# Six of the first layer's weight pieces staged in the tail of the second layer's weights, with a new order for the begin

## The chip, the cores and the metric

The kernel runs on one core of a Trainium2 chip. The metric is the device time of one execution in microseconds (us); three runs of the kernel before gave 632.26, 632.70 and 633.21, median 632.7. The profile is one further execution, of 632.08 us.

## The reference, cut to what matters

A delta-rule attention over 4 batches and 8 heads (768 steps, 48 wide) feeds a two-layer network over its 3072 tokens.

```python
for t in range(S):                                    # 768 steps
    y[:, :, t] = einsum('bhd,bhde->bhe', q[:, :, t], state)
    v_old = einsum('bhde,bhd->bhe', state, k_n[:, :, t])
    state = state + beta_t * einsum('bhd,bhe->bhde', k_n[:, :, t], v[:, :, t] - v_old)
x = y.transpose(0, 2, 1, 3).reshape(3072, 384)
h = x @ w_in                                          # 384 -> 2048
out = (h * cos(h)) @ w_out                            # 2048 -> 384
```

The two weights come as float64.

## The kernel before

**Attention.** The 768 steps are 24 *units* of 32 steps, each for all 32 pairs of batch and head. A unit n is a chain of *tasks*, and the state links unit n to n + 1. Its loads are `k n`, `q n` and `v n` (four DMAs of 48 KB each to unit 7; from unit 8 on `k n` has eight of half the size, and the q and k blocks for the turn come separately). Then: norms of k (`square` on ScalarE (ACT), `sum` on VectorE (DVE), `norms`, a power, on GpSimd (POOL), `scale` on DVE), `turn` (transposes on TensorE (PE), L561; copied out by `turn_out` on ACT), `gram` (PE, L598), read by `gram_keys`, `fold` and `gram_queries` on DVE; the inverse of a unit triangular matrix, for two units at once, in pieces `inv(m, i)` on POOL (L734, L735), for the first two units on DVE, between `cross` and `back` on DVE; `state` (PE, L764); `old` (ACT, L776); `right` (DVE, L787 and L791); for units 0 to 3 `solve_half` (PE, L801), `half_out` (ACT), `between` (PE, L801), `between_out` (DVE, L819), `solve` (PE, L835), for later units only `solve` (L841); `solve_out` (DVE, L849); `update` of the state (PE, L862) and `update_out` (DVE, L870 or L872); `within` (PE, L879), copied out by `within_out` (ACT, L897) and, for units 0 to 3, `within_rest` (DVE, L895); `features`, a transpose (PE, L905), and `features_out` (ACT, L912). From unit 4 on `within_turn` (DVE), `within_put` and `features_out` (both DMAs) take the place of the last two. `busy` tasks are 26 small multiplications (L954) that only keep PE at work in the begin.

**The network.** Two units make a block p of 256 tokens; there are twelve. Blocks 0 and 1 form h by `hidden(p, f)` in eight steps of two halves each (PE, L963, 12 instructions a half); `hidden(0, 0)` needs the first three pieces of w_in, `hidden(0, 6)` all twelve. Each step is gated by `turns` (ACT, L1001), `rest` (DVE, L1008), `cos` (ACT, L1017) and `gate` (DVE, L1026). Block 0 is multiplied by w_out in `out(0, i, k)` (PE, L1169), which need four more pieces of w_out for each k. From block 2 on the first layer goes through sums of x and of weight blocks (`x_sum`, `in_sums` on DVE; `layer`, PE, L1149), and from block 1 on the second through seven products (L1226) with sums of weights (`right(x, e)`, DVE, L1255; not to be taken for the `right` of a unit) and of gates (`left`). `store` is the DMA of a result.

**The weights.** They come in 28 *pieces*: 0 to 11 are w_in (128 x 512 words of 8 bytes, 512 KB each), 12 to 27 w_out (128 x 384, 384 KB, one tile f each). Piece t passes through `weights t` (the load, on SyncE's queue (SP), L454), `split t` (two operations on ACT, L462 and L464), `shift t` (two on DVE, L468 and L473) and `add t` (one on POOL, L477), which makes float32 of it in w_in or w_out. The raw words lie in one of four places, w0 to w3, until their add is done; a load takes the place that came free first.

**What sets the order.** `Order.LINE` lists all 2253 tasks by number. `run` calls them in that order, so each engine and SP's queue get their instructions in the order of the list, and an instruction at the head waits for what it needs while all behind it on its engine wait too. Every DMA on SP also waits until the eighth DMA before it has landed. PSUM banks go in the same way: three for hidden (`h`), one shared (`two`) by turn, gram, the solves, update and features, one (`kq`) for state and within, and for turn and gram of units 1 and 3.

Of the kernel before, what the change touches and what calls it, by code (L numbers as in the profile page):

```python
# [12 lines left out]
U32 = mybir.dt.uint32  # L13
# [187 lines left out]
def kernel(  # L201
# [36 lines left out]
    DM = H * D  # L238
# [1571 lines left out]
```

## Time and profile before

| | us |
|---|---|
| median of three runs | 632.7 |
| the profiled execution | 632.08 |
| its span, first to last instruction | 630.3 |
| PE busy | 601.7 (95%) |
| DVE busy | 546.2 (87%) |
| ACT busy | 352.3 |
| POOL busy | 348.3 |
| mean granted PE clock | 0.985 |

The profile cuts the span into 40 slices of 15.76 us; a digit is an engine's busy share of a slice in tenths. A line of PE, DVE or ACT in order of time has its start, its duration, the source line, what is written and read, and in brackets how long the engine sat idle before it and what ended that wait; "issue" means that the profile shows nothing the engine waited for. SPq is SP's queue; its waits are listed with their total, number and longest.

### The profile page before, as it was taken

The page shows a single profiled execution, that of the slowest core. Times are in us where ns is not written, and L with a number is a line of the kernel's source. Part 1 is how long each engine was busy: PE and PEld are TensorE (multiplying, and loading weights), DVE is VectorE, ACT ScalarE, POOL GpSimd, SP SyncE. Part 2 cuts the span into 40 slices and gives each one's busy share as a digit, 9 for nine tenths or more (in the row PEclk, how much of TensorE's full clock was granted, in tenths as well). Part 3 has the DMA queues.
Part 4 walks back from the last instruction along what each step waited for, and adds up shares of the span by engine and source line. Part 5 has one row for each costly group of instructions (what it writes and reads, how often), then busy time and mean ns, then how long its engine had stood idle before and what let it go on. Part 6 is the DMA issues. An engine that isn't in the chain of part 4 may idle for free.

```text
span 630.3 us, 24280 instructions
## 1 busy us (share of the span) xinstructions
PE 601.7 (95%) x10096; PEld 558.2 (89%) x10096; DVE 546.2 (87%) x1131; ACT 352.3 (56%) x643; POOL 348.3 (55%) x703
## 2 busy tenths in 40 slices
PE   7678899999999999999999999999999999999997
PEld 5557778876999999999999999999999999999996
DVE  7998878999999999998898989989989787878872
ACT  3647566653455755656556656645646645746340
POOL 4467687868758588384286882782683860000000
PEclk9879799999999999999999999999999999999999
DMA  9887474764455645555446335644323203110000
GB/s 184 186 221 175 134 167 111 133 97 88 80 99 96 111 76 103 103 91 103 83 77 132 66 56 110 102 85 86 78 64 81 45 14 65 35 43 21 1 27 25
DMA packets 223986, 57.62 MB, mean 91 GB/s; under 512 B 215684, under 2 KB 218900, under 8 KB 223876
## 3 DMA queue, kind: packets, MB, share of 16 engines
q1 hardware_dynamic: 221444, 55.22, 43.1%
q8 instruction: 80, 1.31, 0.9%
q10 hardware_dynamic: 2176, 0.39, 0.4%
q0 software_dynamic: 256, 0.45, 0.3%
q14 instruction: 30, 0.25, 0.1%
HBM read 42.13 MB, written 13.89 MB: 89 GB/s over the span
## 4 chain that ended last, share of the span: by engine, by line
PE 80%; DVE 8%; DMA 4%; ACT 2%; issue 2%; SPq 2%; POOL 1%; DVEq 0%; ACTq 0%; POOLq 0%
PE p_out L1226 29%; PE p_h L1149 28%; PE p_kq L764 4%; PE p_h L963 3%; PE p_out L1169 3%; PE p_s L862 3%; PE p_kq L879 3%; PE p_g L598 3%; PE p_u L841 2%; DMA pairs<-in_moe_w_in_dram 2%; PE p_o L1226 2%; DMA qp<-in_q_dram 1%; SPq L339 1%; DVE p_h L1047 1%; DVE pairs L468 1%
## 5 line engine op out<-in xcount | busy, mean ns | idle before, releaser
L734 POOL TENSOR_TENSOR part<-z,gb 128x56 f32<-128x56 f32 (+25 forms) x325 | 134.7, 414 | 107.0 <-DMA gb<-g_dr 67.0
L735 POOL TENSOR_TENSOR z<-z,part 128x56 f32<-128x56 f32 (+25 forms) x325 | 140.3, 432 | 25.5
L1165 ACT COPY g_ffn<-p_h 128x512 f32<-128x512 f32 x140 | 80.2, 587 | 91.8 <-DVE p_h L1047 47.4
L1226 PE MATMUL p_out<-w_out,g_ffn 128*128 128x192 f32 x672 | 121.2, 329 | 0.0
L1047 DVE TENSOR_TENSOR p_h<-p_h,g_ffn 128x512 f32<-128x512 f32 x140 | 97.0, 695 | 21.3 <-PE p_h L1149 13.3
L1226 PEld LDWEIGHTS p_out<-w_out,g_ffn 128*128 128x128 f32 x672 | 107.8, 190 | 1.2 <-issue 0.2
L1001 ACT ACTIVATE turns<-p_h,quarter_turn 128x512 int32<-128x512 f32 x96 | 65.8, 688 | 65.5 <-DVE p_h L1047 54.8
L1226 PE MATMUL p_out<-w_sum,g_ffn 128*128 128x192 f32 x496 | 90.8, 331 | 0.0
L1017 ACT ACTIVATE turns<-turns,halfpi 128x512 f32<-128x512 f32 x96 | 69.1, 722 | 38.6 <-DVE turns L1008 37.0
L1149 PE MATMUL p_h<-x_sum,w_in 128*128 128x128 f32 x640 | 83.4, 277 | 0.3 <-ACT g_ffn L1165 0.2
L1226 PEld LDWEIGHTS p_out<-w_sum,g_ffn 128*128 128x128 f32 x496 | 79.5, 190 | 1.6 <-DVE o L1276 0.4
L1149 PEld LDWEIGHTS p_h<-x_sum,w_in 128*128 128x128 f32 x640 | 78.1, 192 | 1.6 <-ACT g_ffn L1165 0.9
L1008 DVE SCALAR_TENSOR_TENSOR turns<-p_h,turns 128x512 f32<-128x512 f32 x96 | 65.1, 682 | 7.2 <-ACT turns L1001 6.6
L1026 DVE TENSOR_TENSOR g_ffn<-turns,p_h 128x512 f32<-128x512 f32 x86 | 58.3, 679 | 8.1 <-ACT turns L1017 8.0
L1242 DVE TENSOR_TENSOR g_ffn<-g_ffn 128x512 f32<-128x512 f32 x88 | 62.2, 716 | 3.7 <-PE p_out L1226 3.5
L1149 PE MATMUL p_h<-x_sum,in_sum 128*128 128x128 f32 x400 | 53.6, 277 | 0.3 <-DVE g_ffn L1026 0.3
L897 ACT COPY y<-p_kq 32x384 f32<-32x384 f32 x88 | 41.4, 470 | 22.1 <-PE p_kq L879 16.6
L1149 PEld LDWEIGHTS p_h<-x_sum,in_sum 128*128 128x128 f32 x400 | 49.5, 192 | 1.2 <-DVE g_ffn L1026 0.6
L963 PE MATMUL p_h<-x_ffn,w_in 128*128 128x128 f32 x384 | 48.1, 280 | 1.1 <-ACT x_ffn L912 0.7
L963 PEld LDWEIGHTS p_h<-x_ffn,w_in 128*128 128x128 f32 x384 | 44.9, 193 | 2.7 <-POOL w_in L477 0.9
L776 ACT COPY rhs<-p_kq 32x384 f32<-32x384 f32 x86 | 40.2, 468 | 5.3 <-PE p_kq L764 2.8
L1149 PE MATMUL p_h<-x_ffn,w_in 128*128 128x128 f32 x320 | 42.8, 278 | 0.1
(133 smaller groups left out, 893.6 us busy)
## 6 DMA issues: line engine op xcount, KB each, us to landing
pairs<-in_moe_w_in_dram SPq DMA_DIRECT2D x12, 512.0 KB
pairs<-in_moe_w_out_dram SPq DMA_DIRECT2D x16, 384.0 KB
gb<-g_dr SPq DMA_DIRECT2D x20, 256.0 KB
vp<-in_v_dram SPq DMA_DIRECT2D x96, 48.0 KB
out_dram<-o SPq DMA_DIRECT2D x23, 192.0 KB
y_dr<-y_t SPq DMA_DIRECT2D x20, 192.0 KB
x_ffn<-y_dr SPq DMA_DIRECT2D x40, 96.0 KB
kp<-in_k_dram SPq DMA_DIRECT2D x128, 24.0 KB
```

Of the source, the lines that this page charges most:

```text
L734: eng.tensor_tensor(out=part, in0=row, in1=times, op=ALU.mult)
L735: eng.tensor_tensor(out=behind, in0=behind, in1=part, op=ALU.subtract)
L963: nc.tensor.matmul(p_h[:, i], w_in[:, t, (4 * k + i) * 128 : (4 * k + i + 1) * 128], moved(p, t, unit), start=(t == 0), stop=(t == KT - 1),)
L1001: nc.scalar.activation(turns[p, f], hidden_of(p, f), AF.Identity, bias=quarter_turn, scale=TURN)
L1008: nc.vector.scalar_tensor_tensor(out=r, in0=hidden_of(p, f), scalar=TURN, in1=t, op0=ALU.mult, op1=ALU.subtract,)
L1017: nc.scalar.activation(r, r, AF.Sin, bias=halfpi, scale=2.0 * math.pi)
L1026: nc.vector.tensor_tensor(out=place(p, f), in0=step_of(rests.pop((p, f)), f), in1=step_of(hidden_of(p, f), f), op=ALU.mult,)
L1047: nc.vector.tensor_tensor(out=out, in0=one, in1=two, op=ALU.add if op == "add" else ALU.subtract)
L1149: nc.tensor.matmul(p_h[:, e], in_block(w)[:, e], form(p, x), start=first and e == 0, stop=True, skip_group_check=True,)
L1165: nc.scalar.copy(block(p, *CHAIN[i][3]), p_hs[p, BANK[i]])
L1226: nc.tensor.matmul(p_o, left(p, part, a)[:, e % 4], right(e, b), start=(e == 0), stop=(e == FT // 2 - 1), skip_group_check=True,)
L1242: nc.vector.tensor_tensor(out=left(p, s, to), in0=left(p, s, one), in1=left(p, s, two), op=op)
```

## The change

**Staging.** Odd pieces of w_in (1, 3, 5, 7, 9, 11) no longer take one of w0 to w3. They are loaded into four places e0 to e3 of 1024 words per partition each, which are the last 4096 of the 6144 words of the w_out tile. These hold tiles f = 5 to 15 of w_out, written by pieces 17 to 27; `split` of these pieces now also waits for the adds of the six odd pieces.

**Order.** The tasks at places 17 to 1080 of the list stand in another order; ahead of them and behind them the list is the same. The last of them run at about 295 us in the profile of before. Each engine has the same tasks as before. In the begin the lists differ as follows (x:y for task x of unit, block or piece y):

| | before | after |
|---|---|---|
| SP | w0 k2 w1 q2 w2 k3 w3 q3 w4 k4 v0 w5 k5 w6 q4 w7 v1 w8 q5 w9 k6 w10 v2 w11 w12 v3 k7 q6 gram_put4 w13 w14 k8 w15 w16 w17 w18 | w0 k2 w1 k3 w2 q2 w3 q3 w4 k4 v0 w5 k5 w6 q4 w7 w8 v1 w9 k6 w10 k7 w11 q5 w12 k8 v2 w13 w14 q6 gram_put4 w15 v3 w16 w17 w18 |
| POOL | norms 0, add 0, 1, norms(1,0), add 3, norms(1,1), add 2, 4, 5, norms 2, add 7, 6, 8, inv(1,0-1), add 10, 12, inv(1,2), add 11, 9, inv(1,3), add 14, 13, norms 3, add 16, 15 | norms 0, norms(1,0), add 0, 3, 1, 2, norms(1,1), norms 2, add 4, 6, 5, 7, 8, 9, inv(1,0-1), add 10, inv(1,2), add 11, 12, inv(1,3), add 13, 14, norms 3, add 15, 17, 16 |
| DVE, from cross 0 | cross0 fold0 inv(0,0) gram_queries1 shift1 inv(0,1) sum(1,0) inv(0,2) fold1 shift3 shift2 inv(0,3) sum(1,1) scale(1,0) back0 gram_keys2 weigh(0,0) fold2 right0 gram_queries2 shift4 shift5 sum(2,0) between_out0 scale(1,1) solve_out0 shift6 shift7 weigh(0,1) update_out0 within_rest0 | cross0 sum(1,0) inv(0,0) fold0 inv(0,1) gram_queries1 inv(0,2) scale(1,0) shift3 shift1 fold1 inv(0,3) sum(1,1) shift2 back0 gram_keys2 weigh(0,0) fold2 right0 gram_queries2 sum(2,0) shift4 between_out0 shift5 solve_out0 shift6 shift7 update_out0 shift8 within_rest0 |
| DVE, on to update_out 1 | shift8 gram_keys3 cross1 scale(2,0) fold3 gram_queries3 shift9 gram_keys4 shift10 gram_queries4 shift12 right1 shift11 rest(0,0) rest(0,2) between_out1 gate(0,0) solve_out1 sum(3,0) weigh(1,0) shift14 update_out1 | scale(1,1) gram_keys3 shift9 gram_queries3 fold3 cross1 shift10 scale(2,0) sum(3,0) gram_keys4 gram_queries4 weigh(0,1) rest(0,0) right1 shift11 gate(0,0) shift12 between_out1 solve_out1 rest(0,2) shift14 shift13 update_out1 |
| ACT, around old 1 | features_out0 split10 split9 old1 split12 turns(0,2) turns(0,0) split11 square3 half_out1 cos(0,0) | split9 features_out0 eye2 split10 square3 old1 split12 turns(0,0) split11 cos(0,0) half_out1 |
| PE | turn2, six busy, turn3, five busy, gram2 ... within0 busy turn4 gram3 busy features0 hidden(0,0) state1 gram4 hidden(0,2) hidden(0,4) solve_half1 | turn2, six busy, gram2, turn3 ... within0 turn4 busy busy gram3 features0 hidden(0,0) state1 gram4 hidden(0,2) hidden(0,4) solve_half1 |

On PE the order from solve_half 1 on differs by swaps of neighbours. Further on, on DVE, in_sums 1, 4 and 8 stand six to ten places earlier, and gates and sums of weights are moved by a few places; on SP `store(0,0)` goes before `v8` and `within_put 4`, and `k10` before `v5` and piece 23.

```diff
     LINE = """
-0 1 2 3 4 5 6 7 2141 8 9 10 11 12 37 13 76 38 14 39 42 34 98 64 15 43 69 65 40 66 70 44 2145 45 99
-67 71 2142 16 47 17 72 2143 2149 128 75 2144 2146 46 77 106 143 2153 201 129 18 101 74 19 2147 2150
...
+0 1 2 3 4 5 6 7 2141 8 9 10 11 12 37 13 38 14 39 42 34 98 64 15 43 69 65 40 66 70 44 2145 16 45 128
+76 17 67 2142 71 47 18 72 101 19 2143 2149 99 75 2146 102 77 103 2153 129 2144 46 78 2150 106 2157
...
-        homes, free = {}, {t: [f"{t}{i}" for i in range(self.bufs[t])] for t in "ghw"}
+        homes, free = {}, {t: [f"{t}{i}" for i in range(self.bufs[t])] for t in "ghwe"}
...
+    EARLY = range(1, 12, 2)
 
     def narrow_load(t):
         _, src, n = narrows[t]
-        pairs = ffn_pool.tile([128, 4, TOK], U32, name="pairs", tag=order.home, bufs=1)
-        words[t] = pairs.rearrange("p a t -> p (a t)")[:, 0 : 2 * n]
+        if t in EARLY:
+
+            at = FT * DM - (4 - int(order.home[1:])) * 4 * TOK
+            words[t] = w_out.rearrange("p f c -> p (f c)").bitcast(U32)[:, at : at + 2 * n]
+        else:
+            pairs = ffn_pool.tile([128, 4, TOK], U32, name="pairs", tag=order.home, bufs=1)
+            words[t] = pairs.rearrange("p a t -> p (a t)")[:, 0 : 2 * n]
         queue("weights", t).dma_start(out=words[t], in_=src)
...
-            x=2, turns=2, g=GATES, w=4, o=2, o_out=2, **{f"xs{i}": 1 for i in range(6)},
+            x=2, turns=2, g=GATES, w=4, e=4, o=2, o_out=2, **{f"xs{i}": 1 for i in range(6)},
...
-            makes=[("w", ("pairs", t))], moves=1.8 * c, due=LOADS + 2 * t)
-        add(("split", t), "ACT", 1.4 * c, lambda: narrow_split(t), [("weights", t)])
+            makes=[("e" if t in EARLY else "w", ("pairs", t))], moves=1.8 * c, due=LOADS + 2 * t)
+        add(("split", t), "ACT", 1.4 * c, lambda: narrow_split(t), [("weights", t)] + (
+            [("add", x) for x in EARLY] if t > 16 else []))
```

144 rows, old and new, of the table LINE are left out of this document.

## The prediction

> **What bounds the kernel now.** I read the page's slices first, then busy time by stretch, then TensorE's (PE's) instructions in order of time, then the queue's waits.
>
> ```profile
> PE   7678899999999999999999999999999999999997
> ...
> DVE  7998878999999999998898989989989787878872
> ...
> PEclk9879799999999999999999999999999999999999
> ```
>
> PE is the bound from about 100 us on and is not full before. The stretches give sizes (columns: length, busy us and instructions of PE, PE loads, DVE, ACT, POOL; granted clock; DMA share; GB/s):
>
> ```profile
> 15.76:31.50 15.74, 9.94 (x104) 8.03 (x104) 14.64 (x51) 9.44 (x22) 7.66 (x6) 0.89 0.81 186
> 31.50:47.30 15.80, 11.76 (x371) 8.86 (x371) 14.25 (x32) 7.38 (x15) 10.65 (x7) 0.78 0.85 221
> 47.30:63.00 15.70, 12.71 (x339) 11.66 (x337) 12.63 (x26) 11.06 (x20) 12.39 (x28) 1.00 0.72 176
> 63.00:78.80 15.80, 13.32 (x333) 12.25 (x334) 13.20 (x24) 8.63 (x21) 10.70 (x13) 0.78 0.48 134
> ...
> 200.00:300.00 100.00, 99.62 (x1691) 94.97 (x1684) 94.03 (x198) 63.59 (x112) 66.57 (x148) 1.00 0.53 98
> ```
>
> Over the span PE is busy 601.7 of 630.3 us, so 28.6 us are idle: 21.5 of them before 110 us (summed by stretch), 5.0 in the last 30, about 2 between. The change keeps the number of instructions on PE and does not touch the order behind some 295 us, so it can gain only what it takes out of those 21.5 us, and some slow clock (0.78 in two stretches). Until 47 us DVE is the fullest (14.64 of 15.74) and the DMA engines are 0.81 to 0.92 busy; after that the chain of unit 1 is what PE waits for:
>
> ```profile
> 58.81 0.93 PE L801 MATMUL p_w<-rhs,halves_z 32*32 32x48 f32 x64 [0.24 <-DVE rhs L791]
> 60.34 0.88 PE L801 MATMUL p_v<-u_half,halves_z 32*32 32x48 f32 x64 [0.60 <-ACT u_half L811]
> 61.89 0.29 PE L835 MATMUL p_u<-u_half,halves_z 32*32 32x48 f32 x8 [0.68 <-DVE u_half L819]
> 64.04 0.80 PE L835 MATMUL p_u<-u_half,halves_z 32*32 32x48 f32 x56 [1.86 <-issue]
> 66.07 1.56 PE L862 MATMUL p_s<-u,kp 64*64 64x96 f32 x32 [1.24 <-DVE u L849]
> ```
>
> Here PE waits five times, once 1.86 us in the middle of solve 1 with no releaser; then update 1 takes 1.56 us at the slow clock, against 0.89 for the same group at 92.79.
>
> **The change, part by part.** All times are in before's span; I follow PE to its next fixed points.
>
> *The staging.* It adds no instruction. Six loads of w_in go to four new places. What that can free is the queue's wait for places:
>
> ```profile
> SPq L454 <- POOL w_in L477: 0.5, 1, 0.5
> ...
> SPq L454 <- POOL w_in L477: 1.7, 2, 1.5
> ```
>
> (36 to 42 and 42 to 48 us), 2.2 us in front of pieces 9, 10 and 11. But each load also waits for the eighth DMA before it, and the DMA engines were 0.93, 0.79 and 0.89 busy in the 4 us stretches from 40 to 52: at most 12 x 0.13 = 1.6 us of transfer can be moved up. New wait: splits 17 to 27 wait for the six odd adds, the last of which ran by 65; split 17 ran at 76.12. Cost nothing; if add 11 came over 10 us later, ACT would stand there with old 2 behind it.
>
> *To solve_half 0 (33.60).* DVE has the same tasks up to weigh(0,0) in another order and no idle time, so its sum stays. One collision goes: cross 0's second operation took 0.99 us at 16.10, beside POOL's first add (from 15.52), and 0.43 alone at 48.05. In the new order add 0 is behind norms(1,0), which waits for sum(1,0), behind cross 0. Shift's second operation beside an add (1.52 at 26.22, usually 0.42) stays once, at shift 1. turn 2 and turn 3 come later (fold 0, fold 1 and q 2 are later), but gram_keys 2 needs them only at 32. **-0.5.**
>
> *To hidden(0,0) (48.23).* between ended at 36.57, between_out 0 started at 37.25, behind shift 5, which now follows it: -0.7. Then scale(1,1) (1.1) and weigh(0,1) (0.5) leave the way to within_rest 0 and shift 8 (1.1) enters it: about 0. turn 4, gram 3 and features 0 follow: -1.2, and turn 4 loses its 0.43 wait, of which I count 0.1. **-1.3 in all, 46.9.**
>
> *To solve_half 1 (58.81).* From 48.23 to 58.56 PE runs hidden(0,0), state 1, gram 4 and four halves of hidden with 0.1 us of gaps, the same list in both, 10.3 us. So 57.3 at best: **-1.5**, the 0.24 wait gone, if right 1 is done by then. Right 1 has a new condition: rest(0,0) now stands before it on DVE and waits for turns(0,0), which on ACT stands behind split 12, which waits for piece 12 to land. Before:
>
> ```profile
> 53.74 0.57 ACT L462 ACTIVATE w_out<-pairs 128x384 f32<-128x384 f32 x1 [0.44 <-DMA pairs<-in_moe_w_out_dram]
> ```
>
> Landing L, then split 1.0, turns 0.7, rest 0.7, right 1.74 (56.91 to 58.65), 0.15 of hand-overs: L + 4.3. Ahead of piece 12 stand as many k, q and v loads as before (k 7 instead of v 2); with up to 1.6 us moved up L is 52.1 to 53.7. I take 52.7: right 1 done at 57.0, just in time.
>
> *To turn 5 (69.43).* The chain is the same; behind solve_out 1, update_out 1 now waits for rest(0,2), shift 14, shift 13 (0.6 + 0.8 + 0.9) instead of sum(3,0), weigh(1,0), shift 14 (1.98 from 65.92 to 67.90): +0.3, hidden by within 1, whose slow 1.87 us ended at 69.43. Left is the 1.86 us stall. Its bounds: 0 and 1.86. Stalls of this kind inside a group on PE in this stretch are 0.55, 0.30, 1.86 and 0.21; I take their mean, 0.73: another -1.1. **-2.6.**
>
> The Trainium skill, "Runtime: NRT & Kernel Launch", Instruction fetch mechanics, says that a sequencer fetches its instructions in 16 KiB blocks over a DMA queue of its own, mostly hidden; the page of the profile has 80 such packets with 1.31 MB, which fits, but 1.86 us would not be hidden. By the rule the stall is none and the sum -1.5 - 1.86 = -3.4, or the first rival's if the slow clock goes with it; by the row it stays and the sum is -1.5.
>
> *From 69 to 295.* PE waits 1.6 us more up to 100 us, then nearly never. The new PE order only swaps neighbours (hidden(0,10) behind solve_half 2, within 3 before gram 6, state 4 behind hidden(1,6)). At solve_half 2 half_out 2 stands behind two cosines (0.7 each) and the moved half of hidden (1.5) covers them. On the queue k 8's eight loads go before pieces 13 and 14, and k 10, which waits for update 2, before v 5 and piece 23; out(0,0,1) is at 116, and add 19 ran at 96.64. store(0,0) now stands before within_put 4; it waits for out(0,0,3), 2.7 us behind within 4, while within_turn 4 is itself behind four in_sums of 0.7 to 0.9. Bounds +2 and -1.6; I take **0**.
>
> **Sum**: 632.08 (span 630.3 and 1.78 around it) - 2.6 = 629.5 for that execution; it is 0.6 below the median of the runs, so for the median 632.7 - 2.6 = **630.1**.
>
> **Rivals.**
> - *The stall and the slow clock go too.* Without the 1.86, turn 5 is 3.5 earlier (update_out 1 then ends last); turn 5 and the half of hidden behind it took 1.90 and 1.67 against 1.03 and 1.53 at full clock (79.50 and 73.84): 1.0 more. -4.5: 628.2. For it: the idle time that precedes the slow clock shrinks; against: the other four waits stay.
> - *Given back.* From 126 to 157.6 DVE is busy 14.40 and 14.98 of 15.8 us. If its new order delivers gates and sums later there, PE, though ahead at 70, waits until DVE is level: 632.7. For it: DVE 94% busy to 300. Against: 2.9 us of DVE's 10.8 between 58.7 and 69.5 were idle, so it can run ahead too. A staging that frees nothing (every load held by the eighth before it) gives L = 53.7, solve_half 1 at 58.2 and -1.7: still not slower.
> - *Piece 12 late: slower.* From L = 54.35 on, right 1 ends later than its 58.65, and each us of L is a us for solve_half 1 on PE, with between_out 1, solve_out 1, shift 13 and 14 queued behind right 1 on DVE. At L = 57.4: +3.0, 635.7. For it: k 7, piece 11 and q 5 stand before it, its place waits for an add, and the margin is only 1.7 us; against: the loads ahead are as many as before.
>
> **Chances.** Forecast (-1.5 to -3.6) 0.40; stall and clock gone 0.18; given back 0.21; piece 12 late, or another DVE wait of that size, 0.21. A measurement can tell about 0.2% (1.3 us): faster 0.58, same 0.21, slower 0.21. The range takes in -6.0 (the first rival and 1.5 of the 1.6 us of waits up to 100) and, above, +2.0 (the bound of the late stretch and the nearer half of the slower case): 626.7 to 634.7.
>
> **What would show it.** Right: hidden(0,0)'s first group near 46.9, L801 of unit 1 near 57.3, turn 5 near 66.8, as much idle time on PE as before from 110 on. Wrong: ACT waiting for a w_out piece past 54.4 with DVE idle in front of rest(0,0) or right 1; waits on PE between 110 and 295 that sum to over 2 us; the stall as long as before, or elsewhere.

## The result and the profile after

The changed kernel takes 635.25 us (median of 17 runs, 632.88 to 639.38) against 632.97 us (median of 17, 631.37 to 635.31) for the kernel before on the same chip: a ratio of 1.0032, 95% interval 1.0016 to 1.0048. It is slower by about 2.3 us, where 2.6 us less were forecast. The profiled execution took 633.2 us (span 631.4, mean granted clock 0.985), one of the shorter ones of its kernel; so its own lines can hold only a part of the difference. All lines of code from L454 on stand 6 lines further down (shift is now L474 and L479, hidden L969, right L797).

The slices of after, as on its page:

```profile
PE   7668888999999999999999999999999999999997
...
DVE  6998868999999999989889889989989787878872
```

and its stretches (the columns as in the prediction):

```profile
31.50:47.30 15.80, 9.86 (x366) 7.87 (x368) 14.95 (x27) 9.33 (x18) 12.35 (x8) 0.89 0.82 226
47.30:63.00 15.70, 13.29 (x358) 12.13 (x348) 13.83 (x32) 10.12 (x20) 11.45 (x27) 1.00 0.72 156
63.00:78.80 15.80, 13.81 (x343) 12.85 (x343) 13.51 (x25) 9.69 (x24) 11.89 (x14) 0.78 0.51 126
...
94.70:110.50 15.80, 13.97 (x286) 12.91 (x284) 13.70 (x23) 12.44 (x26) 12.19 (x21) 1.00 0.57 119
```

From 31 to 47 us PE is emptier than before (9.86 against 11.76), and DVE and POOL are fuller (14.95 and 12.35 against 14.25 and 10.65). From 47 to 79 us PE is a little fuller than before (13.29 and 13.81 against 12.71 and 13.32), as forecast. In the stretch from 94.7 it is 1.83 us short of full; before, the nearest stretch (94.50 to 110.30) was short by 0.62. The chain of unit 1 stands as it did, only its stall is shorter:

```profile
59.22 0.88 PE L807 MATMUL p_w<-rhs,halves_z 32*32 32x48 f32 x64
60.69 0.88 PE L807 MATMUL p_v<-u_half,halves_z 32*32 32x48 f32 x64 [0.59 <-ACT u_half L817]
62.33 0.29 PE L841 MATMUL p_u<-u_half,halves_z 32*32 32x48 f32 x8 [0.76 <-DVE u_half L825]
63.77 1.34 PE L841 MATMUL p_u<-u_half,halves_z 32*32 32x48 f32 x56 [1.15 <-issue]
66.34 1.56 PE L868 MATMUL p_s<-u,kp 64*64 64x96 f32 x32 [1.23 <-DVE u L855]
```

Solve_half 1 begins at 59.22, later than before (58.81), not at 57.3, and turn 5 at 69.26 (before 69.43), not at 66.8. From 110 to 295 us PE is idle for 1.5 us, after 1.1 in before: the loss does not show there. Nobody waits ahead of solve_half 1 for piece 12; ACT splits it at 53.95 with no idle time ahead:

```profile
53.95 0.56 ACT L468 ACTIVATE w_out<-pairs 128x384 f32<-128x384 f32 x1
```

### The profile page after: what moved, and what is told of

It reads as the page before. It is cut to its first block, busy times and chain, and to the rows that moved or that the text cites. A ratio compares the mean times of both kernels' runs of the same rounds, so it can differ in the third digit from the quotient of the medians.

```text
span 631.4 us, 24272 instructions
## 1 busy us (share of the span) xinstructions
PE 598.9 (95%) x10096; PEld 556.6 (88%) x10096; DVE 547.7 (87%) x1131; ACT 352.7 (56%) x643; POOL 344.0 (54%) x703
## 3 DMA queue, kind: packets, MB, share of 16 engines
q8 instruction: 79, 1.29, 0.9%
## 4 chain that ended last, share of the span: by engine, by line
PE 78%; DMA 7%; DVE 5%; ACT 3%; SPq 3%; issue 2%; POOL 1%; DVEq 0%; ACTq 0%; POOLq 0%
PE p_out L1232 28%; PE p_h L1155 27%; PE p_h L969 4%; PE p_kq L770 3%; PE p_s L868 3%; PE p_out L1175 3%; DMA pairs<-in_moe_w_in_dram 3%; PE p_kq L885 2%; PE p_u L847 2%; PE p_g L604 2%; PE p_o L1232 2%; DMA kp<-in_k_dram 1%; DMA vp<-in_v_dram 1%; DMA qp<-in_q_dram 1%; SPq L339 1%
## 5 line engine op out<-in xcount | busy, mean ns | idle before, releaser
L740 POOL TENSOR_TENSOR part<-z,gb 128x56 f32<-128x56 f32 (+25 forms) x325 | 131.5, 405 | 112.6 <-DMA gb<-g_dr 54.3
L741 POOL TENSOR_TENSOR z<-z,part 128x56 f32<-128x56 f32 (+25 forms) x325 | 137.8, 424 | 25.5
L1007 ACT ACTIVATE turns<-p_h,quarter_turn 128x512 int32<-128x512 f32 x96 | 65.9, 688 | 74.8 <-DVE p_h L1053 63.2
L969 PE MATMUL p_h<-x_ffn,w_in 128*128 128x128 f32 x384 | 48.1, 279 | 1.9 <-issue 1.1
L969 PEld LDWEIGHTS p_h<-x_ffn,w_in 128*128 128x128 f32 x384 | 44.5, 192 | 2.4 <-issue 0.9
```

The lines of the kernel that those rows point to most:

```text
L740: eng.tensor_tensor(out=part, in0=row, in1=times, op=ALU.mult)
L741: eng.tensor_tensor(out=behind, in0=behind, in1=part, op=ALU.subtract)
L969: nc.tensor.matmul(p_h[:, i], w_in[:, t, (4 * k + i) * 128 : (4 * k + i + 1) * 128], moved(p, t, unit), start=(t == 0), stop=(t == KT - 1),)
L1007: nc.scalar.activation(turns[p, f], hidden_of(p, f), AF.Identity, bias=quarter_turn, scale=TURN)
```

## The experiments

**How they are compared.** The times of one kernel scatter by 1.5 to 2 us, so I also compare profiles, at places where PE has done the same work in every order used here: features 1, 2 and 3, and the updates 6, 8 and 12 of the state (the start of each one's first group on PE). The stretches and the span of a row are those of one profiled execution. "Begin" runs to features 1. Times in us; the last two columns are medians of the kernel and of the kernel before on the same chip. All but before and e8 have the staging.

| kernel | begin | to f2 | to f3 | to u6 | to u8 | to u12 | to end | span | median | before |
|---|---|---|---|---|---|---|---|---|---|---|
| before | 75.2 | 22.6 | 21.1 | 60.6 | 43.0 | 90.3 | 317.5 | 630.3 | | 632.97 |
| after | 74.1 | 23.1 | 22.6 | 60.4 | 42.5 | 91.6 | 317.0 | 631.4 | 635.25 | 632.97 |
| e1 stage only | 74.2 | 22.8 | 21.1 | 61.0 | 43.1 | 90.3 | 316.8 | 629.3 | 633.71 | 632.33 |
| e2 within_rest 0 first | 75.2 | 22.0 | 24.8 | 60.4 | 42.5 | 91.6 | 316.6 | 633.0 | 635.88 | 632.33 |
| e3 right 3 first | 75.9 | 22.3 | 23.8 | 60.5 | 42.4 | 91.5 | 317.9 | 634.3 | 635.54 | 632.33 |
| e4 both | 76.0 | 22.5 | 24.9 | 60.4 | 42.7 | 95.6 | 317.0 | 639.2 | 636.85 | 632.33 |
| e5 old, then new | 77.8 | 21.8 | 24.2 | 60.4 | 42.5 | 91.4 | 317.8 | 636.0 | 635.78 | 632.97 |
| e6 new, then old | 75.3 | 23.7 | 21.1 | 63.5 | 44.7 | 90.4 | 317.3 | 636.1 | 635.03 | 632.97 |
| e7 adds cut, new | 73.3 | 22.3 | 23.9 | 60.4 | 42.8 | 91.5 | 317.0 | 631.2 | 635.53 | 632.97 |
| e8 adds cut, old | 75.3 | 22.8 | 21.1 | 63.4 | 43.1 | 90.1 | 318.2 | 634.1 | 633.84 | 632.97 |
| e9 only the middle new | 76.2 | 22.2 | 23.0 | 62.4 | 43.2 | 90.1 | 317.6 | 634.7 | 635.35 | 632.16 |
| e10 only the middle old | 75.7 | 23.3 | 21.1 | 61.8 | 42.7 | 95.6 | 316.9 | 637.1 | 638.47 | 632.16 |
| e11 middle and tail old | 75.7 | 23.3 | 21.1 | 61.5 | 42.8 | 91.1 | 317.1 | 632.6 | 634.03 | 632.16 |
| e12 f3 to u8 new | 74.8 | 22.3 | 21.4 | 61.1 | 42.5 | 91.1 | 317.4 | 630.6 | 634.55 | 632.16 |
| e13 store early | 74.0 | 22.5 | 23.1 | 60.4 | 42.7 | 91.0 | 316.8 | 630.5 | 634.41 | 633.21 |
| e14 e10, store early | 73.7 | 23.3 | 21.1 | 64.3 | 42.7 | 90.7 | 317.0 | 632.8 | 635.20 | 633.21 |
| e15 shifts behind | 76.7 | 22.0 | 24.3 | 60.4 | 42.8 | 91.7 | 317.1 | 635.0 | 636.64 | 633.21 |
| e16 both of these | 76.2 | 23.0 | 22.8 | 60.6 | 42.5 | 90.9 | 316.4 | 632.3 | 635.20 | 633.21 |
| e17 PE's middle old | 76.6 | 25.4 | 23.3 | 60.7 | 42.5 | 90.6 | 316.8 | 636.0 | 637.35 | 631.95 |
| e18 the others' middle old | 75.3 | 29.3 | 21.9 | 64.7 | 42.5 | 90.9 | 317.4 | 641.9 | 640.03 | 631.95 |

The orders below are those of LINE, shown as tasks of one engine.

**First theories.** A: the new order loses at two places that the profile of after shows, shift 8 ahead of within_rest 0, and shifts and a gate ahead of right 3. B: the staging loses. In after DVE stands like this at the first place, from solve_out 0 (L855) to within_rest 0 (L901), with POOL's adds beside it:

```profile
37.40 1.02 DVE L855 TENSOR_TENSOR u<-p_u,bz 128x384 f32<-128x384 f32 x2
...
40.09 0.68 DVE L474 SCALAR_TENSOR_TENSOR w_out<-w_out 128x512 uint32<-128x512 uint32 x1
40.69 1.50 DVE L479 TENSOR_SCALAR w_in<-w_in 128x512 uint32<-128x512 uint32 x1
...
43.81 1.51 DVE L479 TENSOR_SCALAR w_in<-w_in 128x512 uint32<-128x512 uint32 x1
45.35 1.13 DVE L901 COPY y<-p_kq 32x384 f32<-32x384 f32 x2
```

```profile
40.24 1.66 POOL L483 TENSOR_TENSOR w_in<-w_in,pairs 128x512 uint32<-128x512 uint32 x1 [0.97 <-DVE w_in L479]
41.87 3.16 POOL L483 TENSOR_TENSOR w_in<-w_in,w_out 128x512 uint32<-128x512 uint32 x2
```

The same two in before:

```profile
39.41 1.02 DVE L849 TENSOR_TENSOR u<-p_u,bz 128x384 f32<-128x384 f32 x2 [0.62 <-PE p_u L835]
...
43.70 1.13 DVE L895 COPY y<-p_kq 32x384 f32<-32x384 f32 x2
```

So the way from the one to the other takes 8.0 us in after and 4.3 in before. A shift's second operation takes 0.41 at 39.75 and 1.50 beside an add. The edits, e1 first, then VectorE's lists of e2 and e3 (e4 has both):

```diff
-LINE of after
+LINE of before
```
```diff
-shift 8
 within_rest 0
+shift 8
...
+right 3
 shift 22
 gate(0,12)
 shift 19
-right 3
```

e1: 

> The staging of the six odd pieces with the old order of all tasks. Theory A (the loss lies in the new order: shifts 6, 7 and 8 on DVE run beside POOL's adds and hold update_out 0 and within_rest 0 back, and four weight tasks stand before right 3): the staging alone costs nothing, 0 +- 0.8 us against the kernel before, hidden(0,0) at 48.2 +- 0.5 and turn 5 at 69.4 +- 0.8 as before. Theory B (the raw words in the tile of w_out cost something, by waits that the list does not show or by slower operations on them): most of the loss, +1.5 to +2.5, and the splits or shifts of odd pieces take longer or later than those of even ones.

e2: 

> The changed kernel with one task moved: within_rest 0 stands before shift 8 on DVE. Theory A: within_rest 0 starts near 43.2 instead of 45.35, gram 3 near 44.5 instead of 46.6, hidden(0,0) near 46.7 instead of 48.7, and the time falls by 1.5 to 2 against the changed kernel, to 0 +- 0.8 against before. Theory B: as slow as the changed kernel, within 0.7.

e3: 

> The changed kernel with one task moved: right 3 stands before shift 22, gate(0,12) and shift 19 on DVE. Theory A: the wait of 1.46 at solve_half 3 goes, solve_half 3 comes at 102.5 to 102.8 instead of 104.0, and the time falls by 1.0 to 1.5. Theory B: as slow as the changed kernel, within 0.7.

e4: 

> Both moves at once. Theory A: they add up, -2.5 to -3.5 against the changed kernel, which is 0.5 to 1.5 faster than before. Theory B: as slow as the changed kernel, within 1.

e1 gives a ratio to before of 1.0005 (0.9977 to 1.0033), and its stretches are those of before: the staging costs and gains nothing that can be told. This interval alone would still hold the whole loss, and e1's median is 1.4 us over before's. But e2, e3 and e4, with the same staging and the new order but for one or two moved tasks, stand 1.8 to 3.1 us over e1 by medians on the same chip. So the order makes most of the loss, and a smaller share of the staging, which is in every kernel here but before and e8, is not excluded. A does no better: e2 (1.0042, 1.0012 to 1.0072), e3 (1.0054, 1.0025 to 1.0083) and e4 (1.0077, 1.0046 to 1.0108) recover nothing. In e2 within_rest 0 still ran at 45.25, where 43.2 was expected. In e3 right 3 is served, and the gate pushed behind it is late instead; PE's waits from 80 to 120 us:

```profile
PE p_h L969 <- DVE g_ffn L1032: 2.9, 1, 2.9
```

So A falls as it was sized: a single place mended only moves the wait.

**Which half of the order.** The two orders were spliced at state 2 (both ways, e5 and e6), and POOL's adds of pieces 4 to 8 were cut to one column in after (e7) and in before (e8), which leaves these weights' adds out.

```diff
-        nc.gpsimd.tensor_tensor(out=w, in0=w, in1=words.pop(t)[:, :, 0], op=ALU.add)
+        n = 1 if 4 <= t <= 8 else w.shape[1]
+        nc.gpsimd.tensor_tensor(
+            out=w[:, 0:n], in0=w[:, 0:n], in1=words.pop(t)[:, 0:n, 0], op=ALU.add
+        )
```

e5: 

> The changed kernel's staging, with the order of before up to the task state 2 and the new order from there on. Theory A2 (the loss lies in the new order behind state 2: hidden half-matmuls moved out of the space ahead of update 2, VectorE idle there, then the shifts of pieces 19 to 22 bunched ahead of the right-hand side of turn 3): 1.5 to 2.5 us over the kernel before, and TensorE idle by about 2 us between 100 and 112 us. Theory B2 (the loss comes from the begin, where shifts 6 to 8 meet GpSimd's additions and everything behind is only later): within 0.7 us of the kernel before, no wait of TensorE over 1 us behind 80 us. Theory C (nothing but the granted clock of the run): no more than the difference of the clocks.

e6: 

> The reverse: the new order up to state 2, the order of before from there on, with the staging. Theory A2: the 1.0 us by which state 2 starts earlier in the profile of the changed kernel is kept, so 0 to 1.2 us under the kernel before. Theory B2: 1.5 to 2.5 us over it. Theory C: as the one before, by the clocks alone.

e7: 

> The changed kernel, but GpSimd's additions for the weight sums of pieces 4 to 8 go over one column only (the sums are then incomplete). It takes away what shifts 6 to 8 run beside. If the 1.5 us shifts are the two engines in each other's way, they take 0.4 to 0.7 us, the rest of within 0 starts 1 to 1.6 us earlier (about 44 us in place of 45.35), and if that is worth its time to the end (theory B2) the kernel is 1.0 to 1.6 us under the changed one; by theory A2 it is within 0.6 us of it, as the wait of solve_half 3 behind 100 us is left.

e8: 

> The same cut in the kernel before, as a control: its shifts 6 to 8 meet fewer additions, so within 0.5 us of the kernel before by either theory. If it gains as much as the cut does in the changed kernel, the cut tells nothing of the order.

e5 loses as A2 said (1.0043, 1.0025 to 1.0062), and its stretch to f3 takes 24.2 us. But e6, which A2 put at before's time or below, loses too (1.0031, 1.0010 to 1.0051), though its stretch to f3 is 21.1 again: its profile lost 3 us between f3 and update 6, with PE waiting 1.4 us for the DMA zt<-z_dr and a granted clock of 0.64 from 136 to 140 us, just behind that wait (1.00 there in before). In e7, the new order with the adds cut, the second operation of shift 6 and the first of shift 7 take 0.42 and 0.69:

```profile
41.88 0.42 DVE L479 TENSOR_SCALAR w_in<-w_in 128x512 uint32<-128x512 uint32 x1
42.22 0.69 DVE L474 SCALAR_TENSOR_TENSOR w_out<-w_out 128x512 uint32<-128x512 uint32 x1
```

so the two engines do hold each other up: from solve_out 0 to within_rest 0 DVE takes 4.7 us in e7 (40.35 to 45.08), where after takes 8.0. Yet e7 shows no gain in time (635.53; 1.0033, 1.0003 to 1.0063), and e8, the control, is at 1.0006 (0.9983 to 1.0029). In e7 solve_out 0 came 3.0 us later than in after, for a reason that no run here shows, so within_rest 0 ran at 45.08 all the same. Its begin is still the shortest of all (73.3 us), but its stretch to f3 takes 23.9 us, after 22.6: what the collisions cost in the begin does not decide the time.

**Which stretch.** Splices of three and four parts: the new order only from state 2 to features 3 (e9), before's order only there (e10) or there and from update 8 on (e11), the new one only from features 3 to update 8 (e12).

```diff
-LINE of after
+LINE of after to state 2, of before to features 3, of after to the end
```

(e10; the others alike.)

e9: 

> With the staging, the order of before, but from state 2 to features 3 the new order (features 1 and features 3 are places at which TensorE has done the same work in every kernel here). In the ten profiles so far the stretch from features 2 to features 3 takes 21.1 us wherever the order of before runs there, and 22.7 to 24.9 us wherever the new one does. Theory A3 (this stretch makes the loss): 22.7 to 24.9 us there, and 1.5 to 3.5 us over the kernel before in time. Theory D (the loss is in no one place; any order that isn't before's own loses by chance of issue and clock): within 1 us of the kernel before, or over it by something that the stretch doesn't show.

e10: 

> The changed kernel, but from state 2 to features 3 the order of before. Theory A3: the stretch from features 2 to features 3 takes 21.1 us again, and the time falls by 1.5 to 3 us under the changed kernel: 632 to 634 us, within 1 us of the kernel before on either side. Theory B2 (the begin makes the loss): 635 us or more.

e11: 

> As the one before, and the order of before again from update 8 on. In the profiles the stretch from update 8 to update 12 takes 90.2 to 90.4 us with the order of before and 91.4 to 91.6 us with the new one. Theory A3 with this second place: 1.2 us under the kernel with only the middle put back, 631 to 633 us, and so up to 2 us under the kernel before. If that stretch doesn't count: the same time as that kernel.

e12: 

> With the staging, the order of before, but from features 3 to update 8 the new order. There the new order took 60.4 us from features 3 to update 6 in all six profiles, the order of before 60.5 to 63.5, and from update 6 to update 8 the new one 42.5, before's 43.0. Theory A3: 0.5 to 1.5 us under the kernel before. Theory D: over it.

e9 loses 1.0061 (1.0036 to 1.0086) with 23.0 us to f3: the middle alone costs, as A3 said. e10 missed by 4.5 us: its stretch is back at 21.1, but the time is 638.47 (1.0091, 1.0068 to 1.0114), with 95.6 us from update 8 to update 12. e11, with the tail of before as well, is 4.4 us under e10, more than the 1.2 expected, and still over before (1.0032, 1.0016 to 1.0049). e12 missed too (1.0032, 1.0010 to 1.0055). There was thus a second place, behind update 8, and every splice pays something of its own, which speaks for theory D. One such price is seen in the traces: right behind features 3, where these kernels go from one order to the other, PE waits for x_ffn, 1.3 us in e9, 1.7 in e10, 1.5 in e11 and 1.2 in e12. Neither whole order has this wait, so the total times of e9 to e12 say less than their stretches.

**The second place: one store.** In e10 ACT stands 5.06 us for a place of o, and PE 2.67 us for ACT; in after ACT stands 2.71 us there and PE waits 0.32 us for it; in before the same instruction waits for PE and for no store. e10 first, then after:

```profile
309.25 0.33 ACT L1269 ACTIVATE o<-p_out 128x192 f32<-128x192 f32 x1 [5.06 <-DMA out_dram<-o]
```
```profile
310.10 1.16 PE L1155 MATMUL p_h<-x_sum,in_sum 128*128 128x128 f32 x8 [2.67 <-ACT g_ffn L1171]
```
```profile
305.02 0.33 ACT L1269 ACTIVATE o<-p_out 128x192 f32<-128x192 f32 x1 [2.71 <-DMA out_dram<-o]
```

SP's queue shows why. First after, then before (start, time that the issues take, what):

```profile
292.27 0.42 SPq L745 DMA_DIRECT2D z_dr<-z  x1
292.79 3.60 SPq L947 DMA_DIRECT2D x_ffn<-y_dr  x4
296.49 1.75 SPq L688 DMA_DIRECT2D g_dr<-g  x3
298.29 2.09 SPq L753 DMA_DIRECT2D zt<-z_dr  x4
300.42 0.59 SPq L1293 DMA_DIRECT2D out_dram<-o  x1
```
```profile
293.10 1.06 SPq L739 DMA_DIRECT2D z_dr<-z  x1
294.25 0.80 SPq L1287 DMA_DIRECT2D out_dram<-o  x1
```

In the new order store(3,0) stands behind features_out 11, gram_put 14 and get 12 (eleven DMAs), and is issued 6 us later; ACT had its place 4.6 us after the issue began in after (300.42 to 305.02), 5.5 in e10 (303.74 to 309.25). The wait of 2.67 us is not all that e10 pays: from 312 to 316 us the granted clock is 0.67 there (1.00 in after), and the group of out behind the wait takes 2.93 us in place of 1.57. e4, whose store is late too, shows the same (PE waits 2.74 us, clock 0.65) and has 95.6 us as well; where ACT stood only 2.5 to 2.7 us for the late store, that stretch is 91.4 to 91.7. One task was moved, in after (e13) and in e10 (e14):

```diff
 put 6
+store(3,0)
 features_out 11
 gram_put 14
 get 12
-store(3,0)
```

In e15 three shifts were moved on DVE, for the first place, and e16 has both moves:

```diff
-shift 21
 gate(0,10)
 update_out 2
 within_rest 2
+shift 21
 rest(0,12)
 shift 20
+gate(0,12)
+right 3
 shift 22
-gate(0,12)
 shift 19
-right 3
```

e13: 

> The changed kernel with one task moved: the store of output tile 3,0 right behind the transfer put 6 on SyncE's queue, where before had it. If the store makes the second loss: ScalarE's wait for it (2.71 us in the profile of the changed kernel) is gone, update 8 to update 12 takes 90.2 to 90.9 us in place of 91.6, the time falls by 0.5 to 1.3 us under the changed kernel, and the longest runs (638 us and more) go. Rival: the stretch is long for the order of TensorE's own groups there; then it stays at 91.4 to 91.6 us.

e14: 

> The kernel with the middle of before put back (638.47 us; its profile has a wait of 2.7 us of TensorE for ScalarE, and ScalarE 5.1 us for the store), with the same one task moved. If the store makes it: 3 to 4.5 us under that kernel, 634 to 635.5 us, and no such wait. Rival (splices lose by themselves): 637 us or more.

e15: 

> The changed kernel with three tasks moved on VectorE: shift 21 from ahead of update 2's state to behind within 2, shifts 22 and 19 from ahead of the right-hand side of turn 3 to behind it. If these make the first loss: the state of update 2 is added at about 92.5 us in place of 95.0, solve_half 3 does not wait for its right-hand side, features 1 to features 3 takes 43.5 to 44.2 us in place of 45.7, and the time falls by 1.5 to 2.2 us under the changed kernel, to 633 to 634 us. Rival (the wait only moves, as when the right-hand side was put ahead of the gates): 45 us or more, and no gain.

e16: 

> Both of these moves in the changed kernel. If both losses are those tasks: 2 to 3.3 us under the changed kernel, 632 to 633.2 us, level with the kernel before or up to 1 us under it. If only one is: what that one gave.

With the store early ACT no longer waits, in e13 as in e16:

```profile
302.76 0.33 ACT L1269 ACTIVATE o<-p_out 128x192 f32<-128x192 f32 x1
```

Update 8 to 12 falls from 91.6 to 91.0 (after to e13), from 95.6 to 90.7 (e10 to e14) and from 91.7 to 90.9 (e15 to e16), and the medians stand over before's of the same chip by 1.2 in place of 2.3 us, 2.0 in place of 6.3 and 2.0 in place of 3.4. For e13 alone the intervals against before overlap (1.0024, 1.0004 to 1.0045, and after's 1.0032); for e14 (1.0042, 1.0016 to 1.0069) against e10 (1.0091, 1.0068 to 1.0114) they all but part. e13 and e14 came out about as expected; e16 did not (632 to 633.2 us expected) and has no more than the store gives. Of runs of 638 us and more, which e13 was to end, after has 2 of 17, e13 and e16 none of 12, but e14 3 of 12. The traces settle that this store makes the wait; about half of the 1.3 us of that stretch in after is left with it gone.

**The first place.** e15 missed: 636.64 us (1.0057, 1.0033 to 1.0081), 24.3 us to f3. Solve_half 3 no longer waits, and PE waits 2.3 us for a gate instead:

```profile
PE p_h L969 <- DVE g_ffn L1032: 2.3, 1, 2.3
```

What lies under it is seen on DVE, first in after, then in before:

```profile
86.46 0.54 DVE L825 TENSOR_TENSOR u_half<-rhs,p_v 128x384 f32<-128x384 f32 x1
89.68 1.02 DVE L855 TENSOR_TENSOR u<-p_u,bz 128x384 f32<-128x384 f32 x2 [2.68 <-PE p_u L841]
...
93.40 0.60 DVE L474 SCALAR_TENSOR_TENSOR pairs<-pairs 128x384 uint32<-128x384 uint32 x1 [1.50 <-POOL part L740]
...
100.63 0.99 DVE L474 SCALAR_TENSOR_TENSOR pairs<-pairs 128x384 uint32<-128x384 uint32 x1
...
102.16 1.12 DVE L793 TENSOR_TENSOR rhs<-vp,p_kq 32x384 f32<-32x384 f32 x2
```
```profile
87.50 0.69 DVE L1026 TENSOR_TENSOR g_ffn<-turns,p_h 128x512 f32<-128x512 f32 x1 [2.08 <-ACT turns L1017]
89.01 0.69 DVE L1008 SCALAR_TENSOR_TENSOR turns<-p_h,turns 128x512 f32<-128x512 f32 x1 [0.82 <-ACT turns L1001]
```

PE's wait for right 3 in after:

```profile
104.00 0.88 PE L807 MATMUL p_w<-rhs,halves_z 32*32 32x48 f32 x64 [1.46 <-DVE rhs L797]
```

DVE is idle for 4.2 us (2.68 and 1.50), first for solve 2 (ahead of which PE itself stands still for 1.14 us inside a group, with no releaser), then for piece 21 (the profile names POOL, but ACT's split 21 ends at 93.31, just ahead of the shift). From the same task, between_out 2 (86.46 and 89.62), to right 3 the kernel before (e1 alike) is idle for 1.5 us, but it stood idle just ahead of that task (2.08 and 0.82). From features 1 to the start of right 3 DVE is idle for 4.6 us in before, 5.3 in after, 4.6 in e9 and 4.2 in e13, and busy for 21.5, 22.8, 22.9 and 23.7. So right 3 is late less for an idle DVE than for 1.2 to 2.2 us more of work ahead of it. The splits of pieces 19 to 22 start at 85.5, 87.4, 88.9 and 93.3 us in before and at 85.5, 90.3, 92.3 and 96.7 in after. From 93.4 to 104 DVE has no gap, and whatever stands last in it is late: right 3, or a gate. All ten profiles with the whole new order here show it: between features 2 and 3 PE waits 1.5 to 2.3 us for right 3 (after, e2, e5, e7, e9, e13) or 2.0 to 2.9 us for a gate (e3, e4, e15, e16), and with before's order no wait of PE there is over 0.4. Where the granted clock stays at 1.00 behind this wait the stretch takes 22.6 to 23.8 us (after, e3, e9, e13, e16); where it falls to 0.60 to 0.79 in one of the next 4 us windows, 23.9 to 24.9 (e2, e4, e5, e7, e15). Two more kernels put back one side of the middle each, with the store early: e17 PE's own list (a half of hidden less ahead of solve_half 2, solve 2 and update 2 in the new one), e18 the lists of all others.

```diff
-PE's tasks of after, from state 2 to features 3
+PE's tasks of before, from state 2 to features 3
```

e17: 

> The changed kernel with store 3,0 early, and TensorE's own order put back to that of before between state 2 and features 3; the other engines keep the new order. If TensorE's order makes the loss (VectorE runs out of work at 87 us, as solve 2 and update 2 come with less hidden work between): features 1 to features 3 takes 43.7 to 44.4 us in place of 45.6, 633 us in all. If the others' order makes it: 45.5 us or more, 634.4 us or more.

e18: 

> The reverse: TensorE keeps the new order, the loads, splits, shifts, gates and GpSimd's tasks go in the order of before between state 2 and features 3, store 3,0 early. If the order of the weight tasks makes the loss: features 1 to features 3 takes 43.7 to 44.4 us in place of 45.6, about 633 us. If TensorE's order makes it: 45.5 us or more.

Both lose: 637.35 (1.0073, 1.0052 to 1.0094) and 640.03 (1.0130, 1.0099 to 1.0160), and from features 1 to features 3 they are the worst of all, with 48.7 and 51.2 us where before has 43.6 and after 45.7. The new order's PE list and the lists of the other engines fit each other better than either fits before's. So neither run tells which side makes the loss of after.

## Why the prediction was wrong, by its steps

- *The staging: nothing.* Right, as far as e1 tells. What it was to free is freed only in part: SP waited 1.6 us for an add between 36 and 48 us, where before had 2.2.
- *To solve_half 0: -0.5.* Right: it starts at 33.3 us on average over the kernels that keep the whole new begin (eleven profiles) and at 33.8 over those with before's (six, e8 among them).
- *To hidden(0,0): -1.3, at 46.9.* This step failed first. It came at 48.69, against 48.23; over the eleven profiles it starts at 49.5 us on average (48.2 to 50.7), over the six at 48.4 (47.3 to 49.1): 1.1 later, not earlier. The term that failed is the "about 0" up to within_rest 0. Solve_out 0 still came 0.8 earlier (38.7 against 39.5 on average), but from it to within_rest 0 DVE took 7.1 to 8.1 us in the eleven and 4.3 to 4.7 in the six: 2.9 more. scale(1,1) was not on that way, as solve_out 0 waited 0.62 for PE behind it, so at usual durations the term is the 1.1 of shift 8 less the 0.5 of weigh(0,1), +0.6. The rest are collisions: with POOL's list moved too, the shifts 6, 7 and 8 met adds and took 1.91, 2.18 and 2.41, and with these adds cut (e7) the way took 4.7.
- *To turn 5: -2.6.* It came at 69.26, where 66.8 was forecast. The stall of solve 1 was sized well in kind and too high in amount: on average 1.5 with before's begin (0.8 to 2.1) and 1.0 with the new one (0.3 to 1.5), so -0.5 and not -1.1. Of the four stalls that I averaged, before's profile has three (0.55, 1.86 and 0.21); no row has the 0.30. By the rule of the Trainium skill that I weighed there ("Runtime: NRT & Kernel Launch", Instruction fetch mechanics) the stall would be gone, and it is not; what it waits for no run here shows. At features 1 the means are 75.6 (74.2 to 77.8, six profiles) and 75.4 (73.7 to 76.7, eleven): the new begin gains 0.2. The scatter of one and the same order is larger than all that I summed from single lines of one execution.
- *Piece 12 late.* Rightly not the likeliest: it was not late, and the time rose by another way.
- *From 69 to 295: 0.* The costlier failure. The profiles of after and before differ by +0.5 to f2, +1.5 to f3 and +1.3 from update 8 to 12, with -0.2 and -0.5 between. Before's own f3 to update 6 is 60.6, 61.0 and 63.4 us in three profiles of the unspliced order (before, e1, e8), so part of its lead is lost in some executions: from features 1 to update 8 these three take 147.2, 148.0 and 150.4 us, and the nine with the new order throughout it (after, e2 to e5, e7, e13, e15, e16) 148.6 to 150.6. I named the moves around 100 us harmless as PE's list "only swaps neighbours"; but in the new order DVE has 1.2 to 2.2 us more work ahead of right 3, and PE waits for it or for a gate. Which of the moves does it is open. I weighed store(0,0), but not store(3,0), which is the one that ACT waits for.
- *Given back.* The rival with the right mechanism, DVE not level with PE, was placed at 126 to 157 us and capped at no change; PE's wait came at 104 us in after and cost more than the begin gained. The range ended at 634.7, half a microsecond short of the result.

What is shown: the order makes most of the loss; the begin gains next to nothing, as shifts and adds collide in it; features 2 to 3 takes 1.5 to 3.8 us more wherever the new order runs there (after, e2 to e5, e7, e9, e13, e15, e16), part of which comes back by update 8; the store costs a part of a microsecond to 4 us. Of the 2.3 us by medians, the two profiles hold 1.1. What stays open: where the longer executions of after lose the rest, whether the staging has a small share, whether one task makes the loss at features 2 to 3 (three tries only moved the wait), and the rest of the stretch from update 8 to 12. No kernel here beats the kernel before.

## What to carry to other kernels

A gain summed from waits of one profiled execution is worth no more than the scatter of that sum between executions: profile an unchanged order two or three times, and compare at places of equal work, before trusting a microsecond. When a planner reorders everything, look at each queue's full list, stores and late transfers too, for a task that went behind others while someone waits for its buffer. A wait mended at the head of a full engine moved to the next task in it (e3, e15). The thing to try next is to take work from that engine there, or to move work into its idle time; no kernel here does.

## What the runs showed of the hardware

A shift's second operation on DVE (128 x 512 words) took 0.41 us alone and 1.50 beside a POOL add of 1.3 to 1.7 us of another piece, and with the adds cut to one column 0.42 each time. The Trainium skill, "SBUF — State Buffer", SBUF: two separate sides, says that VectorE, in a two-port mode or with two inputs in SBUF beside a GpSimd operation that reads it, and GpSimd share one pair of ports as an exclusive lock, held for a whole instruction. The traces agree: the 1.09 us more is less than one add, and the add beside it grew from 1.29 to 1.66.

After some waits of PE the granted clock was lower for some 4 us, and after others as long it was not: 0.67 behind a wait of 2.67 us (e10), 0.64 behind 1.45 (e6), 0.78 behind 2.28 (e2), but 1.00 behind 2.86 (e3), 1.90 (e13) and 1.46 (after). So a wait cost about its own length in some profiles and one to two and a half microseconds more in others.

Splices of two orders that each run well cost up to 8 us (e18) though every engine does the same work. And the issue of one DMA on SP, z_dr<-z, took 0.53 us in before, 0.78 in e6, 1.18 in after and 1.45 in e8 at the same place of the work (122 to 124 us), with PE waiting for zt<-z_dr 1.4 us in e6, 1.2 in e8 and not at all in after.
